# First attention in halves of the queries, first FFN begun on half the tokens, weights in thirds: one change to a fused attention and FFN kernel on one core

## The chip, the cores and the metric

The kernel runs on one core of a Trainium2 chip. The metric is the device time of one execution in microseconds (us). Every execution also has a span (first to last instruction of the core) and a mean granted clock of the matmul engine; the time was 1.9 us above the span in the profiled execution of the kernel before (472.68 against 470.8 us). "PE" is the matmul engine, "ACT" the scalar engine, "DVE" the vector engine, "POOL" the GpSimd engine and "SP" the sync engine, which here only issues DMAs.

## The reference

Eight batches of attention with 12 heads, 448 tokens and head size 64, in which the softmax has one more term in its denominator (a score of zero). Its output, as 3584 tokens of width 768, goes through an RMS normalisation and a gated FFN of inner width 1536.

```python
s = scale * q @ k.T                                   # 8 x 12 x 448 x 448
e = exp(s - m)
x = (e / (e.sum(-1) + exp(-m) + 1e-9)) @ v            # -> 3584 x 768
xn = x / sqrt(mean(x * x) + 1e-6) * rms_g
g, val = xn @ w_gate, xn @ w_val                      # 768 -> 1536
out = (g * sigmoid(g) * val) @ w_out                  # 1536 -> 768
```

## The kernel before

A batch is 448 tokens, handled as C = 4 pieces of P = 112. Heads go in pairs, six pairs a batch. For each pair q and k are transposed on PE ("turned"), four score groups are made and exponentiated on ACT, and two groups of sums (exponentials times v) follow. The first batch's attention stands alone at the start; from the second batch on, attention is woven between the FFN matmuls of earlier batches by a table of times in emission order.

```python
C = 4; P = S // C; NP = H // 2          # 4 pieces of 112 tokens, 6 pairs of heads
WB = DFF // 2                           # gate and value weights come in halves
NQPE = 7                                # groups of q, k (4 heads each) that PE turns; later ones go by DMA
stage = ctx.enter_context(tc.tile_pool(name="stage", bufs=2))     # q_f, k_f, v_f of later groups
ps_s = ctx.enter_context(tc.tile_pool(name="ps_s", bufs=2, space=bass.MemoryType.PSUM))  # scores
ps_u = ctx.enter_context(tc.tile_pool(name="ps_u", bufs=2, space=bass.MemoryType.PSUM))  # sums, turns
ps_f = ctx.enter_context(tc.tile_pool(name="ps_f", bufs=2, space=bass.MemoryType.PSUM))  # FFN
# ...
def emit_T(g):                          # turn a pair
    n, j = divmod(g, PG)
    ps = ps_u.tile([128, 2, C, P], BF16, name="qkt_ps", tag="u")
    # ... 16 transposes
    t = pair_bufs[g % 3]                # a tile for each pair
    nc.vector.tensor_copy(out=t[:, :, 0:S], in_=ps.rearrange("p i c t -> p i (c t)"))
    pair_t[g] = t
# ...
def ahead(n, jj):                       # loads of groups three ahead, on SP's queue
    n += AHEAD
    if NPE * NG + NG <= n < B * NG:     # from group 9 on
        if jj == 0:
            for i in range(3):
                load_qkv(n, i, nc.sync)
# ...
def warm(n):                            # n dummy matmuls
    ps = ps_f.tile([128, 512], FP32, name="warm_ps", tag="f")
    for _ in range(n):
        nc.tensor.matmul(ps, lhsT=blank[:, 0:128], rhs=blank, start=True, stop=True)
# ...
    warm(10)
    emit_T(0)
# ...
    between = {                         # what follows each group of scores (pair, piece)
        (0, 0): [lambda: emit_T(1)],
        (0, 1): [gains, lambda: [load_qkv(2, i, G) for i in range(2)], lambda: warm(1)],
        (0, 2): [lambda: cast_qkv(0, 2, V), lambda: load_qkv(2, 2, G), lambda: warm(1)],
        (0, 3): [lambda: warm(1)],
        (1, 0): [lambda: warm(1)],
        (1, 1): [lambda: emit_AV(0, 0)],
        # ...
    }
    for g in range(NP):
        for c in range(C):
            scores(g, c)()
            for f in between[g, c]:
                f()
    emit_AV(NP - 1, 0)
    emit_AV(NP - 1, 1)
    scale_w(1, A)
    emit_root(0)                        # 1 / rms of all 448 tokens
    # ...
    warm(14)
    for c in range(C):
        emit_scale(0, c)
    # ... turns of x, weights scaled by the gain; then the FFN
```

The softmax here doesn't subtract the row's maximum and nothing guards it: scores larger than these inputs give would overflow.

## Time and profile before

| | before |
|---|---|
| time, median of 3 | 475.81 us (473.4 to 476.49) |
| span of the profiled execution (its time: 472.68 us) | 470.8 us |
| PE busy | 456.7 us, 97% |
| the 24 exponentials of the first batch | 7.95 to 27.78 us |
| first FFN matmul | at 35.57 us |
| from there to the end of the span | 435.2 us |

The page of the kernel before: first its busy times, then busy tenths of PE in 40 slices of 11.8 us, and the granted clock in the same slices.

```profile
PE 456.7 (97%) x4048; PEld 246.7 (52%) x4048; DVE 241.1 (51%) x621; ACT 249.1 (53%) x365; POOL 95.8 (20%) x109
...
PE   7989998999999999999999989999999999999996
...
PEclk9999999999999999999999999999999999999999
```

The matmul engine is the limit nearly everywhere. The few slices below 9 are the start and the tail, and the start is what the change is about.

The timeline of ACT of the kernel before, 7 to 29 us. Columns: start, duration, engine, line, operation, out<-in, count; in brackets, idle time just before and what ended it.

```profile
7.95 3.34 ACT L210 ACTIVATE p_sb_108<-s_ps 112x896 bf16<-112x896 f32 x4 [4.30 <-PE s_ps L205]
11.17 3.35 ACT L210 ACTIVATE p_sb_111<-s_ps 112x896 bf16<-112x896 f32 x4
14.36 3.39 ACT L210 ACTIVATE p_sb_114<-s_ps 112x896 bf16<-112x896 f32 x4
...
24.44 3.34 ACT L210 ACTIVATE p_sb_114<-s_ps 112x896 bf16<-112x896 f32 x4 [0.22 <-PE s_ps L205]
```

Four exponentials take 3.22 us from one line's start to the next, with hardly any brackets: ACT is the limit of the first 28 us (busy 19.6 of the 19.8 us from 7.95 to 27.78), and PE has some slack (18.4 us busy). After the last exponential another 7.8 us pass before the FFN begins (last sums, squares, root, scalings, transposes).

### The profile page before, as it was taken

Reading aid. Unit: us, or ns where it says so; the run is one execution under the profiler, and the core shown is the slowest. Engines: PE = TensorE matmul, PEld = TensorE weight load, DVE = VectorE, ACT = ScalarE, POOL = GpSimd, SP = SyncE. Lnnn points to the kernel's source line nnn. Section 1 sums busy time; section 2 is a strip of 40 time slices with the busy share of each in tenths; the row PEclk is TensorE's granted clock in tenths of the full one; section 3 lists DMA queues with packets and bytes.
Section 4 is the critical chain, followed back from the end, with each engine's and each line's share of the span. In section 5 each row is a group of like instructions: output and inputs, shape, how many; then the busy total and the mean of one; then the engine's idle time right before and its main releaser. Section 6 shows DMA issues by size and latency. Waiting matters only on the chain.

```text
span 470.8 us, 9822 instructions
## 1 busy us (share of the span) xinstructions
PE 456.7 (97%) x4048; PEld 246.7 (52%) x4048; DVE 241.1 (51%) x621; ACT 249.1 (53%) x365; POOL 95.8 (20%) x109
## 2 busy tenths in 40 slices
PE   7989998999999999999999989999999999999996
PEld 3644544555555554544555544545455555555563
DVE  5676699455541276656532166755643247555200
ACT  4977764656555665545456555555556652222221
POOL 8424455123020222131011210313000000000000
PEclk9999999999999999999999999999999999999999
DMA  8999974998099894693069796289015221100133
GB/s 134 225 227 190 209 189 101 233 240 156 1 221 170 225 194 114 121 227 66 0 145 194 198 203 144 52 176 181 4 36 127 69 68 24 36 1 0 36 100 100
DMA packets 86776, 60.47 MB, mean 128 GB/s; under 512 B 50646, under 2 KB 81692, under 8 KB 86732
## 3 DMA queue, kind: packets, MB, share of 16 engines
q1 hardware_dynamic: 73820, 43.60, 42.5%
q0 software_dynamic: 12912, 16.26, 18.6%
q8 instruction: 31, 0.51, 0.5%
q14 instruction: 13, 0.11, 0.1%
HBM read 47.19 MB, written 11.01 MB: 124 GB/s over the span
## 4 chain that ended last, share of the span: by engine, by line
PE 85%; DVE 9%; ACT 4%; issue 1%; POOL 0%; DVEq 0%; ACTq 0%
PE o_ps L334 24%; PE v_ps L309 21%; PE g_ps L309 16%; PE u_ps L235 9%; PE s_ps L205 8%; PE s_ps L309 5%; DVE xsq L261 3%; DVE x_sb L239 1%; ACT p_sb_108 L210 1%; DVE ht_sb L320 1%; PE warm_ps L353 1%; ACT t_sb L313 1%; PE qkt_ps L178 1%; ACT p_sb_114 L210 1%; DVE x_sb L266 1%
## 5 line engine op out<-in xcount | busy, mean ns | idle before, releaser
L309 PE MATMUL v_ps<-xnt_sb,wv_bf 128*128 128x448 bf16 x576 | 125.0, 353 | 2.4 <-DVE ht_sb L320 2.4
L334 PE MATMUL o_ps<-wo_bf,ht_sb 128*128 128x384 bf16 x672 | 116.5, 326 | 0.0
L309 PE MATMUL g_ps<-xnt_sb,wg_bf 128*128 128x448 bf16 x444 | 96.4, 353 | 0.7 <-DVE silu_4291 L315 0.6
L334 PEld LDWEIGHTS <-ht_sb 128*128 128x128 bf16 x672 | 62.6, 98 | 46.2 <-issue 7.8
L309 PEld LDWEIGHTS <-wv_bf 128*128 128x128 bf16 x576 | 52.8, 97 | 54.5 <-issue 10.9
L309 PEld LDWEIGHTS <-wg_bf 128*128 128x128 bf16 x576 | 52.2, 97 | 54.2 <-issue 11.2
L313 ACT ACTIVATE t_sb<-g_ps 128x448 f32<-128x448 f32 x74 | 40.3, 544 | 68.7 <-PE g_ps L309 68.6
L210 ACT ACTIVATE p_sb_108<-s_ps 112x896 bf16<-112x896 f32 x64 | 55.5, 915 | 15.6 <-PE s_ps L205 15.5
L210 ACT ACTIVATE p_sb_114<-s_ps 112x896 bf16<-112x896 f32 x64 | 56.0, 919 | 11.8 <-PE s_ps L205 11.8
L337 ACT ACTIVATE out_sb<-o_ps 128x384 f32<-128x384 f32 x56 | 27.5, 491 | 65.6 <-PE o_ps L334 56.2
L210 ACT ACTIVATE p_sb_111<-s_ps 112x896 bf16<-112x896 f32 x64 | 55.7, 918 | 9.5 <-PE s_ps L205 9.5
L238 DVE RECIPROCAL recip<-u_ps 112x4 f32<-112x4 f32 x96 | 17.0, 177 | 82.7 <-PE u_ps L235 82.7
L239 DVE TENSOR_TENSOR x_sb<-u_ps,recip 112x256 bf16<-112x256 f32 x96 | 40.7, 424 | 3.3
L154 POOL CAST q_bf<-q_f 112x1024 bf16<-112x1024 f32 x17 | 17.7, 1040 | 102.7 <-DMA q_f<-in_q_dram 83.9
L292 POOL TENSOR_TENSOR rinv<-ms,neghalf 112x4 f32<-112x4 f32 x8 | 8.3, 1032 | 146.4 <-DVE ms L286 141.5
L205 PE MATMUL s_ps<-qk_t 64*128 64x448 bf16 x272 | 37.5, 354 | 0.0
L261 DVE CUSTOM_DVE_ANT_0 xsq<-x_sb 112x256 bf16<-112x256 bf16 (+3 forms) x62 | 35.2, 568 | 1.6
L313 ACT ACTIVATE t_sb<-s_ps 128x448 f32<-128x448 f32 x22 | 12.0, 544 | 38.5 <-PE s_ps L309 33.3
L309 PE MATMUL s_ps<-xnt_sb,wg_bf 128*128 128x448 bf16 x132 | 28.6, 352 | 0.0
L235 PEld LDWEIGHTS <-p_sb_114 112*128 112x128 bf16 (+1 forms) x512 | 19.8, 97 | 6.7 <-issue 1.4
L235 PEld LDWEIGHTS <-p_sb_111 112*128 112x128 bf16 (+1 forms) x512 | 20.0, 97 | 5.7 <-issue 1.2
L235 PEld LDWEIGHTS <-p_sb_108 112*128 112x128 bf16 (+1 forms) x512 | 19.3, 98 | 6.8 <-issue 2.8
(278 smaller groups left out, 383.0 us busy)
## 6 DMA issues: line engine op xcount, KB each, us to landing
q_f<-in_q_dram SPq DMA_DIRECT2D x15, 448.0 KB, 5.0
k_f<-in_k_dram SPq DMA_DIRECT2D x15, 448.0 KB, 6.3
v_f<-in_v_dram SPq DMA_DIRECT2D x15, 448.0 KB, 7.4
v_f<-in_v_dram POOLq DMA_DIRECT2D x9, 448.0 KB, 9.1
out_dram<-out_sb SPq DMA_DIRECT2D x8, 336.0 KB, 2.8
wg_bf<-in_moe_w_gate_dram POOLq DMA_DIRECT2D x2, 1152.0 KB, 16.5
wv_bf<-in_moe_w_val_dram POOLq DMA_DIRECT2D x2, 1152.0 KB, 14.3
wo_bf<-in_moe_w_out_dram POOLq DMA_DIRECT2D x3, 768.0 KB, 14.9
```

Source lines behind the costliest of these rows:

```text
L154: eng.tensor_copy(out=dst, in_=staged[n, i].rearrange("p h c d -> p c h d"))
L205: nc.tensor.matmul(s_ps[:, hh, 0:S], lhsT=k_t[r, k0:k0 + 128], rhs=qs[r], start=True, stop=True)
L210: nc.scalar.activation(out=p_v, in_=s_ps[0:P, :, 0:S], func=AF.Exp, scale=scale)
L235: nc.tensor.matmul(u_ps[:, qc, :], lhsT=p_sb[0:K, q0:q0 + 128], rhs=v_sb[0:K, c, h, :], start=(c == 0), stop=(c == C - 1))
L238: nc.vector.reciprocal(out=recip, in_=u_ps[0:P, :, D:E1])
L239: nc.vector.tensor_tensor(out=x_tiles[b][:, :, h * D:(h + 1) * D], in0=u_ps[0:P, :, 0:D], in1=recip.to_broadcast([P, C, D]), op=ALU.mult)
L261: nc.vector.tensor_tensor_reduce(out=xsq[:, 0:n], in0=x_c, in1=x_c, scale=1.0, scalar=0.0, op0=ALU.mult, op1=ALU.add, accum_out=acc)
L292: nc.gpsimd.tensor_tensor(out=rinv, in0=ms, in1=neghalf, op=ALU.pow)
L309: nc.tensor.matmul(ps[:, 0:S], lhsT=w[:, dk, m * 128:(m + 1) * 128], rhs=xnt_tiles[b][:, :, dk, :], start=(dk == 0), stop=(dk == KD - 1))
L313: nc.scalar.activation(out=t, in_=ps[:, 0:S], func=AF.Tanh, scale=0.5)
L334: nc.tensor.matmul(o_ps[:, 0:HN], lhsT=ht_tiles[b2][:, fk, c * 128:(c + 1) * 128], rhs=wo_bf[:, fk, n * HN:(n + 1) * HN], start=(fk == 0), ...
L337: nc.scalar.activation(out=o_sb[:, n * HN:(n + 1) * HN], in_=o_ps[:, 0:HN], func=AF.Copy, scale=0.5)
```

## The change

Intent: do the first batch's attention in two halves of the queries. Once half of the tokens have all heads, they are normalised, turned, and given to the FFN while the other half is finished, so that the FFN begins sooner. For this a unit of work is a pair of heads and half of the queries; k is needed by both halves, so q and k of a pair stay in a tile that two pairs share; the gate and value weights come in thirds, so that the first third is scaled in time; the sums get one PSUM buffer and the FFN three; and the second batch's attention is placed anew.

```diff
-    WB = DFF // 2
+    WB = DFF // 3
-    NQPE = 7
+    NQPE = 8
-    ps_u = ctx.enter_context(tc.tile_pool(name="ps_u", bufs=2, space=bass.MemoryType.PSUM))
-    ps_f = ctx.enter_context(tc.tile_pool(name="ps_f", bufs=2, space=bass.MemoryType.PSUM))
+    ps_u = ctx.enter_context(tc.tile_pool(name="ps_u", bufs=1, space=bass.MemoryType.PSUM))
+    ps_f = ctx.enter_context(tc.tile_pool(name="ps_f", bufs=3, space=bass.MemoryType.PSUM))
@@ def turned(n):
-            nc.vector.memset(qkt[n][:, :, LQ:], 0.0)
+            nc.vector.memset(qkt[n] if n < NG else qkt[n][:, :, LQ:], 0.0)
@@ def emit_T(g):
-        ps = ps_u.tile([128, 2, C, P], BF16, name="qkt_ps", tag="u")
+        ps = ps_f.tile([128, 2, C, P], BF16, name="qkt_ps", tag="f")
+        if g < NP:
+            dst = turned(n)[:, :, 0:LQ].rearrange("p i (c j t) -> p i c j t", c=C, j=PG)
+            for i in range(2):
+                nc.vector.tensor_copy(out=dst[:, i, :, j, :], in_=ps[:, i, :, :])
+            return
@@ new: scores of two key pieces for one half of the queries, sums of one half
+    def scores_half(g, h, cp, k):
+        # ... four matmuls of 224 columns, one exponential of 896 columns
+    def sums_half(g, h, k):
+        u_ps = ps_u.tile([128, 2, 2, E1], FP32, name="u_ps", tag="u")
+        # ... 16 matmuls, then reciprocal and multiply into x_sb on DVE
+    def emit_A_half(mm, part, h):
+        # ... two blocks of 128 FFN columns for 224 tokens in one PSUM buffer: 12 matmuls
@@ the x turns of the second half, and weights, now behind the FFN's start (cut)
+    ops.append((3.3, lambda: (emit_turn_x(0, 2), emit_turn_x(0, 3))))
-    for j, t0 in enumerate((0.0, 2.3, 4.9, 7.5, 11.6, 14.2, 18.4, 22.5)):
+    for j, t0 in enumerate((4.5, 7.0, 13.0, 14.5, 15.8, 17.1, 20.0, 25.5, 30.5, 36.0)):
         ops.append((t0, lambda j=j: emit_T(NP + j)))
@@ the first batch: twelve units instead of six pairs
+    units = [(0, 0), (1, 0), (0, 1), (1, 1), (2, 0), (3, 0), (2, 1), (4, 0), (5, 0), (3, 1), (4, 1),
+             (5, 1)]
     between = {
+        (2, 1): [lambda: sums(0)],
+        (3, 0): [lambda: sums(1)],
+        (3, 1): [lambda: emit_T(2), lambda: load_w(2), lambda: cast_qkv(1, 2, G)],
+        (4, 0): [lambda: emit_T(3)],
+        # ...
+        (10, 1): [lambda: emit_turn_x(0, 0), lambda: emit_stats(0, 0, (3,))],
+        (11, 0): [lambda: sums(10), lambda: emit_turn_x(0, 1)],
+        (11, 1): [lambda: scale_w(2, V)],
     }
+    # ... after the last unit: sums, squares and root of the second half
+    warm(6)
```

## The prediction

> **What bounds it now.** The matmul engine: 456.7 of 470.8 us busy, the chain of waits 85% on it. From 85 us to the tail it idles 2.5 us (busy time by stretch: 368.5 of 371), so three places can give: the first 35.6 us, 35.6 to 85, and the tail.
>
> - 7.9 to 27.8 (timeline): the first batch's 24 exponentials run back to back on the scalar engine, 0.81 us apart. It is busy 19.6 of 19.9 us.
> - 27.8 to 35.6 (timeline, chain of waits): last sums, squares, root (1.15 us on GpSimd), scalings, transposes, 14 dummy matmuls. The first FFN matmul is at 35.57.
> - 35.6 to 85: FFN and second batch's attention. Its pieces (24 groups of six at 1.14, 14 score groups at 0.48, 12 sums at 0.50, 13 turns) sum to 46 of 49.5 us.
> - Tail: last eviction ends at 466.7, span at 470.8: one output DMA.
>
> **What changes.** The first half of the queries is normalised, scaled and turned while the last exponentials run. FFN work on it follows after some weight scaling and six dummies: about 2.2 us after the last exponential instead of 7.8. Gross gain about 5.5 us. [...]
>
> **What it costs.**
> 1. Each turned pair is now copied into a shared tile whose two pairs interleave; the built program makes the next scores wait for that copy, even for the other pair. Turn 0.51 + copy about 0.7 + scores 0.3 + latencies = 1.7 us (from the trace) against 0.8 per exponential: five such places, 0.5 to 0.9 us each. The last exponential moves from 27.8 to about 30 to 31.5. This eats 2 to 4 us of the gain.
> 2. Work moved behind the FFN's start: two transposes of the second half (0.8 us) and one turn (0.5).
> 3. Two more turns on the matmul engine: 1.0 us.
> 4. Second batch's attention is squeezed: about 26 us of matmul work against about 25 us scalar and 26 us vector. Loss 0 to 2 us over before.
>
> **Gains beside.** Three instead of two FFN PSUM buffers: most of the 2.4 us that matmuls waited for ht/silu. Output tail by halves: about 0.7 us. One buffer for the sums should be harmless later (1.6 us of other matmul work lies between sums). Weights in thirds should arrive in time (210 GB/s now).
>
> Sum: -5.5 +3 +1.3 +1.0 +0.5 (squeeze) -2 -0.7, so about -2.5 to -3. All of it is on the critical path.
>
> **Predicted: 473.0 us, 468.5 to 477.0 (80%). Faster by over 2%: 0.04; within 2%: 0.93; slower: 0.03.**
>
> **What would show it.** First FFN matmul at 32 to 34 us (35.6 before), about 2 us after the last exponential. Scalar idle of 2 to 4 us between the first 24 exponentials, released by scores that waited for the qk_t copies. Waits for ht_sb on matmuls near zero. Tail after last eviction near 3.4 us.
>
> **What would make it wrong.** If copies hide under the scores' two buffers, the first FFN matmul comes at 30 and the time is about 470. If the squeezed stretch stalls (vector engine's queue, single sums buffer), or third weights or keys land late, 476 to 478.

The terms as they stand come to -2.4 us, recorded as about -2.5 to -3.

## More of the kernel before

The timeline of PE of the kernel before, from the start.

```profile
1.20 4.45 PE L353 MATMUL warm_ps<-blank 128*128 128x512 bf16 x10 [1.20 <-DVE blank L65]
5.58 0.58 PE L178 MATMUL qkt_ps<-identity,q_bf 112*64 112x112 bf16 x8
...
7.54 0.36 PE L205 MATMUL s_ps<-pair_t_102 64*128 64x448 bf16 x2 [1.01 <-DVE pair_t_102 L181]
```

Ten dummy matmuls, a first turn, 1.01 us idle, then scores. The same turn of eight takes 0.58 us here and 0.36 to 0.39 from 7.84 us on: the array is at half rate at first. The durations show it (so do the ten dummies here, 0.445 us each, where the 14 at 28.76 us took 0.228); the granted clock row does not (it gives 1.00 from time zero).

Waits of PE in the kernel before, 36 to 125 us (us in total, times, longest).

```profile
PE v_ps L309 <- DVE ht_sb L320: 0.9, 3, 0.4
PE u_ps L235 <- DVE pair_t_102 L181: 0.6, 1, 0.6
PE xnt_ps L275 <- DVE x_sb L266: 0.4, 1, 0.4
PE s_ps L205 <- DVE pair_t_106 L181: 0.2, 1, 0.2
```

Once the FFN runs, PE waits about 2 us in 89.

## The result, and the profile after

| | before | after |
|---|---|---|
| time, median | 475.84 us (4 runs) | 496.0 us (4 runs, 495.17 to 497.31) |
| span | 470.8 us | 494.0 us |
| last of the first 24 exponentials ends | 27.78 us | 47.12 us |
| first FFN matmul | 35.57 us | 50.47 us |
| first FFN matmul to end of span | 435.2 us | 443.5 us |

The ratio is 1.0435 (95% interval 1.0399 to 1.0472): slower. Ratios are the mean time of one kernel's fast runs over that of the other's of the same rounds, so not quite the ratio of the medians quoted. The prediction of 473.0 us, and its range up to 477.0, are missed by far.

In the two traces the loss has two parts: 14.9 us before the first FFN matmul, where a gain of about 2.5 was expected, and 8.3 us after it, where nothing or a small gain was expected. Together 23.2 us of span.

The page of the kernel after, the same lines.

```profile
PE 466.8 (94%) x4169; PEld 255.6 (52%) x4169; DVE 248.8 (50%) x644; ACT 250.8 (51%) x362; POOL 96.1 (19%) x110
...
PE   6777988779999999999999999999999999999996
...
PEclk9975999999999999999999999999999999999999
```

The hole is in the first eight slices (12.35 us each). The granted clock falls in the third and fourth. No slice of the profile before had that.

ACT's timeline of the kernel after, 10 to 47 us.

```profile
10.80 0.92 ACT L251 ACTIVATE p_sb_108<-s_ps 112x896 bf16<-112x896 f32 x1 [6.20 <-PE s_ps L247]
13.04 0.92 ACT L251 ACTIVATE p_sb_108<-s_ps 112x896 bf16<-112x896 f32 x1 [1.32 <-PE s_ps L247]
...
30.95 0.92 ACT L251 ACTIVATE p_sb_108<-s_ps 112x896 bf16<-112x896 f32 x1 [1.77 <-PE s_ps L247]
...
46.20 0.92 ACT L251 ACTIVATE p_sb_110<-s_ps 112x896 bf16<-112x896 f32 x1 [1.12 <-PE s_ps L247]
```

One exponential costs what it did (0.92 us; 915 to 919 ns on the page before). Nearly each now has a bracket: ACT waits for scores. The first starts 2.85 us late. From the first exponential to the last ACT is busy 21.9 of 36.3 us (19.6 of 19.8 before): it idles 14.4 us, where the prediction had 2 to 4. PE is busy 26.4 of them, so the limit has gone from ACT to PE and the waits in front of PE.

The first DMAs of SP's queue, after (before, the first line was the only one in the first 20 us):

```profile
0.75 0.38 SPq L570 DMA_DIRECT2D rms_rows<-in_moe_rms_g_dram  x1
1.20 0.35 SPq L151 DMA_DIRECT2D q_f<-in_q_dram  x1
1.58 0.48 SPq L151 DMA_DIRECT2D k_f<-in_k_dram  x1
```

These are q and k of group 9, 448 KB each, needed much later. In the old program they were third in line for a pool of two buffers and waited for the pool. With NQPE at 8 one group fewer passes through that pool, group 9 finds a free buffer, and its DMAs start at 1.20 us (80.20 us before), ahead of q and k of the very first pair, of which q is issued at 1.30 us. PE's timeline from the start shows the result:

```profile
7.66 0.58 PE L186 MATMUL qkt_ps<-identity,q_bf 112*64 112x112 bf16 x8 [2.02 <-DMA q_bf<-in_q_dram]
...
8.81 1.46 PE L432 MATMUL warm_ps<-blank 128*128 128x512 bf16 x3
10.21 0.56 PE L247 MATMUL s_ps<-qk_t 64*128 64x224 bf16 x4
```

The first turn is 2.08 us late, and the scores at 10.21 take 0.56 us for what takes 0.36 at full rate.

Later in the same timeline:

```profile
28.31 0.36 PE L186 MATMUL qkt_ps<-identity,k_bf 112*64 112x112 bf16 x8
30.48 0.36 PE L247 MATMUL s_ps<-qk_t 64*128 64x224 bf16 x4 [1.81 <-DVE qk_t L191]
...
31.02 0.59 PE L186 MATMUL qkt_ps<-identity,k_bf 112*64 112x112 bf16 x8
32.39 0.55 PE L247 MATMUL s_ps<-qk_t 64*128 64x224 bf16 x4 [0.79 <-DVE qk_t L191]
```

The scores at 30.48 waited 1.81 us for a copy into the shared tile; DVE was filling (memset) other tiles meanwhile, the last of them the shared tile of the next two pairs:

```profile
28.51 0.82 DVE L169 MEMSET qk_t<- 128x912 uint32 x1
...
29.74 0.68 DVE L191 COPY qk_t<-qkt_ps 128x448 bf16<-128x448 bf16 x2
```

The turn behind it is already slow (0.59 us at 31.02 for the 0.36 of 28.31), and the array runs at half rate from there, until about 50 us.

PE's waits, after, 7 to 51 us, then 51 to 125 us:

```profile
PE s_ps L247 <- DVE qk_t L191: 5.0, 5, 1.8
PE u_ps L264 <- DVE x_sb L269: 2.1, 5, 0.5
PE qkt_ps L186 <- DMA q_bf<-in_q_dram: 2.0, 1, 2.0
PE xnt_ps L328 <- DVE x_sb L319: 1.6, 1, 1.6
...
```

```profile
PE xnt_ps L328 <- DVE x_sb L319: 2.1, 1, 2.1
PE u_ps L288 <- DVE x_sb L292: 1.6, 3, 0.9
PE s_ps L218 <- ACT p_sb_110 L223: 1.4, 4, 0.4
PE v_ps L361 <- DVE wv_bf L129: 1.3, 2, 1.0
PE v_ps L361 <- ACT wv_bf L127: 0.9, 1, 0.9
PE g_ps L361 <- DVE xnt_sb L333: 0.8, 1, 0.8
...
```

In the second stretch the waits listed for the kernel after sum to 9.9 us (with the four lines cut, of 0.6, 0.5, 0.5 and 0.2), against 2.1 before. The waits for ht_sb are gone, as predicted; others have come. The 12 matmuls of 224 columns are innocent: a group starts at 52.09 and the next at 53.24, so one takes 96 ns, about half of the 190 ns of one of 448 columns before (six from 35.57 to 36.71 us). Only the very first group was still at half rate (50.47 to 52.09, 1.62 us).

### The profile page after: what moved, and what is told of

Its sections match the earlier page's. It is cut to its first block, busy times and chain, and to the rows that moved or that the text cites. A ratio compares the mean times of both kernels' runs of the same rounds, so it can differ in the third digit from the quotient of the medians.

```text
span 494.0 us, 10113 instructions
## 1 busy us (share of the span) xinstructions
PE 466.8 (94%) x4169; PEld 255.6 (52%) x4169; DVE 248.8 (50%) x644; ACT 250.8 (51%) x362; POOL 96.1 (19%) x110
## 4 chain that ended last, share of the span: by engine, by line
PE 88%; DVE 5%; ACT 3%; DMA 1%; issue 1%; POOL 0%; ACTq 0%; POOLq 0%
PE o_ps L411 23%; PE v_ps L361 21%; PE g_ps L361 16%; PE u_ps L288 8%; PE s_ps L218 7%; PE s_ps L361 5%; PE u_ps L264 2%; PE s_ps L247 2%; PE warm_ps L432 1%; PE qkt_ps L186 1%; DMA k_bf<-in_k_dram 1%; PE g_ps L384 1%; DVE qk_t L191 1%; DVE xsq L314 1%; DVE x_sb L269 1%
## 5 line engine op out<-in xcount | busy, mean ns | idle before, releaser
L361 PE MATMUL v_ps<-xnt_sb,wv_bf 128*128 128x448 bf16 x552 | 120.3, 353 | 2.7 <-DVE wv_bf L129 1.3
L361 PE MATMUL g_ps<-xnt_sb,wg_bf 128*128 128x448 bf16 x420 | 91.2, 353 | 0.8 <-DVE xnt_sb L333 0.8
L361 PEld LDWEIGHTS <-wv_bf 128*128 128x128 bf16 x552 | 50.2, 98 | 52.9 <-issue 7.9
L223 ACT ACTIVATE p_sb_110<-s_ps 112x896 bf16<-112x896 f32 x56 | 49.4, 916 | 10.8 <-PE s_ps L218 10.8
L223 ACT ACTIVATE p_sb_109<-s_ps 112x896 bf16<-112x896 f32 x56 | 48.9, 915 | 10.2 <-PE s_ps L218 10.2
L291 DVE RECIPROCAL recip<-u_ps 112x4 f32<-112x4 f32 x84 | 14.8, 177 | 75.2 <-PE u_ps L288 75.2
L223 ACT ACTIVATE p_sb_108<-s_ps 112x896 bf16<-112x896 f32 x56 | 48.8, 915 | 7.6 <-PE s_ps L218 7.3
L345 POOL TENSOR_TENSOR rinv<-ms,neghalf 112x4 f32<-112x4 f32 (+1 forms) x9 | 8.6, 959 | 159.9 <-DVE ms L343 133.6
L162 POOL CAST q_bf<-q_f 112x1024 bf16<-112x1024 f32 x16 | 16.7, 1042 | 106.6 <-DMA q_f<-in_q_dram 90.9
L292 DVE TENSOR_TENSOR x_sb<-u_ps,recip 112x256 bf16<-112x256 f32 x84 | 35.7, 424 | 3.2 <-DMA q_f<-in_q_dram 0.4
L314 DVE CUSTOM_DVE_ANT_0 xsq<-x_sb 112x512 bf16<-112x512 bf16 (+1 forms) x61 | 35.0, 574 | 1.6
L218 PE MATMUL s_ps<-qk_t 64*128 64x448 bf16 x256 | 35.3, 354 | 0.0
L288 PEld LDWEIGHTS <-p_sb_110 113*128 113x128 bf16 x448 | 17.5, 97 | 6.1 <-DVE x_sb L292 1.9
L288 PEld LDWEIGHTS <-p_sb_108 113*128 113x128 bf16 x448 | 17.0, 97 | 6.8 <-issue 1.9
L288 PEld LDWEIGHTS <-p_sb_109 113*128 113x128 bf16 x448 | 17.5, 97 | 5.5 <-issue 1.1
```

The costliest lines, as they stand in the source:

```text
L162: eng.tensor_copy(out=dst, in_=staged[n, i].rearrange("p h c d -> p c h d"))
L218: nc.tensor.matmul(s_ps[:, hh, 0:S], lhsT=k_t[r, k0:k0 + 128], rhs=qs[r], start=True, stop=True)
L223: nc.scalar.activation(out=p_v, in_=s_ps[0:P, :, 0:S], func=AF.Exp, scale=scale)
L288: nc.tensor.matmul(u_ps[:, qc, :], lhsT=p_sb[0:K, q0:q0 + 128], rhs=v_sb[0:K, c, h, :], start=(c == 0), stop=(c == C - 1))
L291: nc.vector.reciprocal(out=recip, in_=u_ps[0:P, :, D:E1])
L292: nc.vector.tensor_tensor(out=x_tiles[b][:, :, h * D:(h + 1) * D], in0=u_ps[0:P, :, 0:D], in1=recip.to_broadcast([P, C, D]), op=ALU.mult)
```

## The experiments

The theory after reading: three independent holdups of PE (the early loads; the tile shared by two pairs; one buffer for the sums) each leave PE idle for 0.4 to 2 us, the array's rate halves on such idleness, and at half rate PE's work for one exponential exceeds ACT's 0.81 us, so PE becomes the limit. The trace of before shows two rates: its first ten dummies took 0.445 us each, the 14 at 28.76 us 0.228. That idleness brings the lower one was the theory at this point, and the runs below test it. Rivals: one of the holdups alone does it; the rate is a bystander; and for the loss behind the FFN's start, that the second batch's attention is packed too densely.

Eighteen kernels were run. The summary, with the ratio to before in its own rounds; "rest" is the span from the first FFN matmul to the end.

| run | based on | median us | ratio (95%) | first FFN matmul | rest |
|---|---|---|---|---|---|
| before | | 475.8 | | 35.57 | 435.2 |
| after | | 496.0 | 1.044 (1.040, 1.047) | 50.47 | 443.5 |
| hold | after | 494.0 | 1.042 (1.039, 1.045) | 48.33 | 443.6 |
| early_before | before | 477.2 | 1.007 (1.004, 1.010) | 39.07 | 436.0 |
| dummies | after | 491.1 | 1.036 (1.033, 1.040) | 44.54 | 444.3 |
| hold_pairs | after | 490.1 | 1.034 (1.029, 1.038) | 45.24 | 443.4 |
| u2 | after | 499.6 | 1.052 (1.048, 1.057) | 44.09 | 453.1 |
| hold_pairs_u2 | after | 492.1 | 1.036 (1.032, 1.040) | 37.14 | 453.4 |
| spread | after | 497.6 | 1.048 (1.044, 1.051) | 50.24 | 443.8 |
| fix | hold_pairs_u2 | 488.3 | 1.029 (1.025, 1.034) | 35.79 | 450.5 |
| fix_u | fix | 483.8 | 1.020 (1.016, 1.023) | 35.42 | 445.2 |
| fix_u_w | fix_u | 481.2 | 1.016 (1.012, 1.021) | 36.65 | 443.0 |
| best | fix_u_w | 477.8 | 1.007 (1.004, 1.010) | 34.57 | 441.4 |
| best_w | best | 478.3 | 1.008 (1.005, 1.011) | 34.10 | 442.0 |
| tail_before | before | 475.0 | 1.001 (0.998, 1.003) | 37.90 | 435.0 |
| before_cold | before | 474.9 | 1.001 (0.998, 1.004) | 38.17 | 435.5 |
| before_warm | before | 472.9 | 0.996 (0.994, 0.999) | 35.55 | 435.7 |
| hold_dummies | after | 491.5 | 1.036 (1.033, 1.038) | 46.12 | 443.8 |
| hold_u2 | after | 495.5 | 1.044 (1.040, 1.048) | 42.30 | 451.5 |
| before_u1 | before | 477.4 | 1.007 (1.004, 1.011) | 39.27 | 435.7 |

The first FFN matmul and the rest come from one trace of each, so small steps in these two columns are not clear of scatter. Kernels that are the same up to the first FFN matmul show how much: after and spread differ by 0.2 us, best and best_w by 0.5, fix_u and fix_u_w by 1.2, before and tail_before by 2.3.

### The early loads: hold and early_before

hold puts the q and k of group 9 on GpSimd's queue, where they come late (after 100 us):

```diff
                 for i in range(3):
-                    load_qkv(n, i, nc.sync)
+                    load_qkv(n, i, G if n == NPE * NG + NG and i < 2 else nc.sync)
```

> The changed kernel, with the first two loads of the hardware DMA queue (queries and keys of the tenth group, 448 KB each) issued from GpSimd's queue in their turn instead of at 1.2 us. Theory EARLY LOADS (they compete with the first queries and keys and so start the clock's fall): the first turn begins near 5.6 us instead of 7.66, the first exponential near 8 instead of 10.8, the granted clock is 1.00 up to 20 us; at the least 3 to 5 us come back (491 to 493 us). If the second clock drop (29 to 52 us) hangs on that first one too, the first FFN matmul is at 37 to 39 instead of 50.5 and the time 481 to 484. Theory SHARED TILE alone (idle behind the copies of turned pairs is the cause): the second drop stays, 491 to 493. If neither, 496.

early_before gives the old kernel the early loads: q and k of group 7 are asked for on SP's queue, where nothing holds them.

```diff
-                 (14.3, lambda: (cast_qkv(NG + 2, 2, G), loads(2 * NG + 1))),
+                 (14.3, lambda: (cast_qkv(NG + 2, 2, G), load_qkv(2 * NG + 1, 0, nc.sync),
+                         load_qkv(2 * NG + 1, 1, nc.sync), load_qkv(2 * NG + 1, 2, G))),
```

> The kernel before, with the queries and keys of the eighth group issued from the hardware DMA queue, where nothing holds them back, instead of from GpSimd's queue: it puts the same two early loads into the old kernel. Theory EARLY LOADS: first turn at about 7.6 instead of 5.6 us, half clock from about 9 to 17 us, time 3 to 5 us longer (479 to 481). If only the landing is late and the clock holds, plus 2 us. If the early loads do not matter, the time stays within 0.5 us of before.

In hold the first turn came at 5.25 us, as early as before, yet the first FFN matmul came only 2.1 us sooner. PE's timeline of hold says why:

```profile
12.18 0.37 PE L247 MATMUL s_ps<-qk_t 64*128 64x224 bf16 x4
14.03 0.68 PE L264 MATMUL u_ps<-v_sb,p_sb 113*128 113x65 bf16 x16 [1.48 <-DVE x_sb L269]
...
14.93 0.47 PE L186 MATMUL qkt_ps<-identity,q_bf 112*64 112x112 bf16 x8
15.18 0.59 PE L186 MATMUL qkt_ps<-identity,k_bf 112*64 112x112 bf16 x8
16.56 0.55 PE L247 MATMUL s_ps<-qk_t 64*128 64x224 bf16 x4 [0.79 <-DVE qk_t L191]
```

With the first cause gone, the next took its place: sums waited 1.48 us for the single buffer to be emptied (DVE was filling tiles), and the rate halved within 1 us. In the changed kernel the array was at full rate from 17 us until 30.8. In the old kernel the early loads left PE idle for 1.6 us before the first turn, the clock fell, and the FFN started at 39.07; the time rose by 0.7%. The expectation held there (rate at half from 9.3 to 16 us, 3.3 us more than the median of its rounds), though not the 479 to 481 us. Of hold's, only the early turn did: 494.0 us is above its 491 to 493, and the clock fell at 15 us. In the timed runs hold (1.042) cannot be told from after (1.044). So the early loads are shown to cost by early_before; that they take about 2 us in the changed kernel is the reading of one trace of each. The rest of the span of early_before stayed at 436.0.

### Is it the rate? dummies, hold_dummies, before_cold, before_warm

dummies keeps the array busy with matmuls of nothing, 19 instead of 10 at the start and 3 or 7 behind each turn:

```diff
-    warm(10)
+    warm(19)
     emit_T(0)
-        (3, 1): [lambda: emit_T(2), lambda: load_w(2), lambda: cast_qkv(1, 2, G)],
+        (3, 1): [lambda: emit_T(2), lambda: warm(3), lambda: load_w(2), lambda: cast_qkv(1, 2, G)],
         # the same behind emit_T(1), emit_T(3) and emit_T(5); warm(7) behind emit_T(4)
```

> The changed kernel with more dummy matmuls and nothing else: 19 instead of 10 at the start, three more behind each turned pair of the first batch (seven behind the fifth). Theory CLOCK (the idle itself is short; the halved clock that follows it is what costs): granted clock 1.00 or close to it up to 50 us, the first FFN matmul at 38 to 42 instead of 50.5 us, time 484 to 488. If the idle waits themselves are the cost, more work on the matmul engine cannot help: 495 to 500.

The granted clock stayed at 1.00 until 40 us, and the FFN started 5.9 us earlier although PE had more to do. So the rate is not a bystander here. But 44.5 and 491.1 us lie between the ranges of both theories, and 44.5 is far from 33: the waits for tiles hold the exponentials at full rate too, and the dummies cost time themselves.

hold_dummies is both edits together.

> The changed kernel with the ninth group's q and k put back on GpSimd's queue (as in hold) and the extra dummies (as in dummies). If early loads and lost matmul rate are two separate causes and together most of the late FFN start, the first FFN matmul comes at 38 to 42 (50.5 changed, 48.3 hold, 44.5 dummies), the rest of the span stays at 443 to 445, time 484 to 488. If the shared tile's waits and the single sums buffer are what holds the exponentials whatever the rate, it stays at 43 to 45 and the time at 489 to 491.

It started the FFN at 46.12, later than dummies, and missed both ranges for that point. Nineteen dummies were sized for late loads; with loads in time they stand in front of the first turn (first exponential at 9.76 us instead of 7.03 in hold), and the clock fell anyway, at 16.7 us, behind a wait of 1.27 us for the sums buffer. (In dummies the same wait of 1.27 us, at nearly the same place, lost nothing.) The time of 491.5 is just above where the second theory had put it. Dummies treat a symptom, and blindly added ones are work.

before_cold takes the single dummies out of the old kernel's first scores, and nothing else:

```diff
-        (0, 2): [lambda: cast_qkv(0, 2, V), lambda: load_qkv(2, 2, G), lambda: warm(1)],
-        (0, 3): [lambda: warm(1)],
-        (1, 0): [lambda: warm(1)],
+        (0, 2): [lambda: cast_qkv(0, 2, V), lambda: load_qkv(2, 2, G)],
+        (0, 3): [],
+        (1, 0): [],
         # likewise behind (0, 1), (2, 0), (3, 0) and (5, 0)
```

> The kernel before without the six single dummy matmuls among its first scores, nothing else changed. Theory (a short stretch with an idle matmul engine at the start keeps or drops its rate, and a slow matmul engine then holds up the exponentials): matmuls in 8 to 20 us run slower, the last exponential ends 0.5 to 4 us later than 27.8, first FFN matmul at 36 to 39, rest of the span as before (435 to 436); time 1 to 3 us above before. Rival (the rate of the matmuls does not matter in this kernel, the scalar engine has slack to hide it): last exponential at 27.8, time within 0.5 us. A fall that feeds itself, as in the changed kernel, would show as an FFN start past 42.

(The expectation says six; the edit takes out seven.) Busy times by stretch, PE first and the granted clock before the last two columns:

```profile
5.00:10.00 5.00, 3.02 (x39) 1.58 (x36) 3.11 (x8) 1.41 (x2) 3.79 (x8) 0.75 1.11 184
10.00:15.00 5.00, 4.18 (x44) 2.12 (x41) 1.43 (x3) 4.48 (x6) 3.06 (x5) 0.50 1.29 226
15.00:20.00 5.00, 5.00 (x78) 3.16 (x77) 2.58 (x7) 3.97 (x6) 1.64 (x3) 0.73 1.15 231
```

In this trace about 10 us run at half rate; the last exponential ends at 30.39 instead of 27.78, the first FFN matmul comes at 38.17, 2.6 us late, and the span is 2.9 us longer. Then it recovers: the old order has no other holdup that would feed the loss. So lost rate alone costs 2 to 3 us, not 15.

But it was not the missing dummies that lost it. PE's timeline of before_cold:

```profile
1.19 3.73 PE L353 MATMUL warm_ps<-blank 128*128 128x512 bf16 x10 [1.19 <-DVE blank L65]
4.85 0.39 PE L178 MATMUL qkt_ps<-identity,q_bf 112*64 112x112 bf16 x8
...
7.53 0.55 PE L205 MATMUL s_ps<-pair_t 64*128 64x448 bf16 x2 [1.98 <-DVE pair_t L181]
```

The first scores are at half rate already, ahead of the first dummy taken out. The same ten dummies took 3.73 us here and 4.45 in the profile of before: the array got to full rate sooner, was done sooner, and then idled 1.98 us instead of 1.01 for the copy that comes at 7.5 in either case. So the point at which full rate comes differs between executions of the same start. In a third trace of this start (tail_before, below) the dummies took 4.32 us, the gap was 1.51 us, and the array was at half rate from 8.8 us.

The timed runs gave a ratio of 1.0006, and that too is about the kernel before. Its executions come with their granted clock, and the twelve of these rounds sort themselves: the four with a mean clock of 0.999 took 472.68 to 473.54 us, the three with 0.996 to 0.998 took 474.08 to 474.26, and the five with 0.990 to 0.992 took 474.93 to 476.22. The old kernel seems to lose rate in most executions, and in the traces of the variants that start as it does (before_cold, tail_before) it is at this gap. Its profiled execution, 470.8 us with a clock of 1.000, was one of the lucky ones, so the prediction started from a first stretch some 2 us better than usual. (This also is why the medians differ by 20.2 us and the spans by 23.2.)

before_warm adds three dummies to the old kernel, in this gap:

```diff
     warm(10)
     emit_T(0)
+    warm(3)
```

> The kernel before with three more dummy matmuls after the first turn of q and k. Theory (the old kernel stands near the edge of losing its matmul rate at the start, and loses it in some executions): time 0 to 1.5 us below before, with less spread. Rival (the dummies only stand in the way of the first scores): 0 to 1.5 us above before.

Six executions of 472.1 to 473.34 us, all with a clock of 0.998 to 1.000, idle time before the first scores 0.78 us: ratio 0.9964 (0.9942 to 0.9987). That is 0.36% and well under a per cent, but the interval excludes 1. It is the only version here that beat the kernel before, and the test of the reading above.

How long an idle time loses the rate is not fixed in these runs. fix_u and fix_u_w (below) are the same program up to the first FFN matmul, and in both a turn of x waits 1.73 us. PE's timeline of fix_u, then of fix_u_w:

```profile
29.41 0.47 PE L323 MATMUL xnt_ps<-identity,x_sb 112*128 112x112 bf16 x6 [1.73 <-DVE x_sb L314]
...
29.00 0.74 PE L323 MATMUL xnt_ps<-identity,x_sb 112*128 112x112 bf16 x6 [1.73 <-DVE x_sb L314]
```

In fix_u the turn ran at full rate, and the granted clock fell 2.3 us after the wait, at 31.7 us; in fix_u_w it fell within the wait, at 28.2. The FFN started at 35.42 and 36.65. Which of the two an execution gets is luck as far as these runs tell.

### The shared tile and the sums buffer: hold_pairs, u2, hold_u2, hold_pairs_u2

hold_pairs gives each pair its own tile again, as before, on top of hold. DVE's fills of the whole shared tiles (0.82 us each) go with them, so the step below is that of the tiles and their fills together:

```diff
-        if g < NP:
-            dst = turned(n)[:, :, 0:LQ].rearrange("p i (c j t) -> p i c j t", c=C, j=PG)
-            for i in range(2):
-                nc.vector.tensor_copy(out=dst[:, i, :, j, :], in_=ps[:, i, :, :])
-            return
         t = pair_bufs[g % 3]
@@ scores_half
-        qs = qkt[n][:, 0, 0:LQ].rearrange("p (c j t) -> p c j t", c=C, j=PG)[:, 2 * h:2 * h + 2, j, :]
+        qs = pair_t[g][:, 0, 2 * h * P:(2 * h + 2) * P]
-            k0 = ((2 * cp + cc) * PG + j) * P
+            k0 = (2 * cp + cc) * P
-                                 lhsT=qkt[n][r, 1, k0:k0 + 128], rhs=qs[r], start=True, stop=True)
+                                 lhsT=pair_t[g][r, 1, k0:k0 + 128], rhs=qs[r], start=True, stop=True)
```

> As hold, and each turned pair of the first batch is copied into a tile of its own, as the kernel before does (three tiles in turn are enough); the whole-tile memsets go with it. Theory SHARED TILE on top of EARLY LOADS: three of the five waits of scores for copies go, the last exponential ends at 29 to 31 us instead of 47.1, no half clock, first FFN matmul at 32 to 34, time 478 to 482. If the single sums buffer is what starves the scalar engine in the first attention, the last exponential stays beyond 33 and the time above 486.

u2 gives the changed kernel two sums buffers and two for the FFN and the turns, nothing else:

```diff
-    ps_u = ctx.enter_context(tc.tile_pool(name="ps_u", bufs=1, space=bass.MemoryType.PSUM))
-    ps_f = ctx.enter_context(tc.tile_pool(name="ps_f", bufs=3, space=bass.MemoryType.PSUM))
+    ps_u = ctx.enter_context(tc.tile_pool(name="ps_u", bufs=2, space=bass.MemoryType.PSUM))
+    ps_f = ctx.enter_context(tc.tile_pool(name="ps_f", bufs=2, space=bass.MemoryType.PSUM))
```

> The changed kernel with two PSUM buffers for the attention sums and two for the FFN, as before the change. Theory SINGLE SUMS BUFFER (with one buffer each second sum waits for the vector engine, 0.44 us or more each time; this keeps the matmul engine under-used and the clock at half): the waits of sums for x_sb vanish, first FFN matmul at 46 or earlier instead of 50.5, time at most 492. If the clock falls all the same by the early loads and the copies: gain under 2.5 us (494 to 496).

hold_pairs_u2 joins the three edits (hold, own tiles, two sums buffers).

> hold_pairs with two sums buffers as well: all three suspects of the first attention undone. In hold_pairs the clock fell at about 14 us, right after 1.15 us of waiting for the one sums buffer. If those three together are the cause, the granted clock stays 1.00 to 40 us, the last exponential ends at 29 to 31, the first FFN matmul is at 32 to 34 (45.2 in hold_pairs), time 476 to 479. If the clock still falls, the first FFN matmul is beyond 40.

hold_u2 is hold with two sums buffers, and so differs from hold_pairs_u2 in the shared tiles and their fills alone.

> The changed kernel with the early q and k loads held back and two buffers for the sums (two for the FFN and the turns), its first batch still turned into the shared tiles. It differs from hold_pairs_u2 (first FFN matmul at 37.1) in the shared tiles alone. If these cost what the prediction said (2 to 4 us on the last exponential) and no more, the FFN starts at 39 to 41. If they cost more, because the waits of up to 2 us at the matmul engine halve its rate as well, 42 to 44. If nothing, 37 to 38, and the early loads and the single sums buffer explain all. Rest of the span 453, time 493 to 498.

Own tiles on top of hold (hold to hold_pairs) bring the FFN's start from 48.33 to 45.24, not to the expected 32 to 34; the rate still fell at about 14 us, behind a wait of 1.15 us for the sums buffer, and the branch that named this buffer came true (time above 486). Two sums buffers alone (after to u2) bring it from 50.47 to 44.09, as expected; the time of 499.6 was not. Put one upon the other they form a ladder, in which the steps depend on the order taken:

| undone, one upon the other | first FFN matmul | step |
|---|---|---|
| nothing (after) | 50.47 | |
| early loads (hold) | 48.33 | -2.1 |
| single sums buffer (hold_u2) | 42.30 | -6.0 |
| shared tiles (hold_pairs_u2) | 37.14 | -5.2 |

Three edits take back 13.3 of the 14.9 us. The last of them, hold_pairs_u2, still missed its expectation (32 to 34 us, clock 1.00 to 40 us): the clock fell at about 29 us, while a turn of x waited 1.73 us. The waits for shared tiles in hold_u2 (PE, 5 to 40 us) were these, the longest (2.17 us, before the scores at 23.76 us) at the place where in after DVE was filling a whole tile:

```profile
PE s_ps L247 <- DVE qk_t L191: 5.9, 5, 2.2
```

The granted clock in 20 to 30 us was 0.76 in hold_u2 and 0.96 in hold_pairs_u2. PE waited 1.9 us for copies of turned pairs in hold_pairs_u2, against these 5.9. So the waits seem to be most of the step, and the rate part of it. The start of the FFN at 42.30 was in the range of the theory that both act.

But the time hardly moved (492.1 us in hold_pairs_u2, 490.1 in hold_pairs): with two FFN buffers the rest of the span grew from 443.5 to 453. Turns of pairs and of x had been moved by the change into the FFN's pool, and two buffers are too few for both.

### The rest of the span: spread, before_u1, fix, fix_u, fix_u_w

spread places the second batch's pairs evenly, in case the dense placing was what cost:

```diff
-    for j, t0 in enumerate((4.5, 7.0, 13.0, 14.5, 15.8, 17.1, 20.0, 25.5, 30.5, 36.0)):
+    for j, t0 in enumerate((4.5, 7.0, 10.2, 12.8, 15.2, 17.4, 20.0, 25.5, 30.5, 36.0)):
-    for j, t0 in enumerate((5.6, 8.6, 14.1, 15.5, 16.9, 18.3)):
-        ops += [(t0 + 0.34 * i, op) for i, op in enumerate(micro_ops(NP + j))]
+    for j, t0 in enumerate((5.6, 8.2, 10.8, 13.4, 16.0, 18.3)):
+        ops += [(t0 + (0.34 if j == 5 else 0.6) * i, op) for i, op in enumerate(micro_ops(NP + j))]
```

> The changed kernel, only the second batch's attention is spread evenly over the first FFN (a pair each 2.6 us of the plan instead of two pairs, a pause and four pairs each 1.4). Theory SQUEEZE (scalar and vector engine are overloaded in the dense part): the 443.5 us from the first FFN matmul to the end fall to 439 to 441, time 492 to 494. If the loss lies in the halves themselves and the moved turns, it stays at 443 to 444 and the time at 496.

The rest was 443.8 against 443.5. Placing them evenly gained nothing; the theory that the density is the cause, which the prediction had named as a risk, falls.

before_u1 gives the old kernel the change's PSUM buffers, and nothing else:

```diff
-    ps_u = ... bufs=2 ...
-    ps_f = ... bufs=2 ...
+    ps_u = ... bufs=1 ...
+    ps_f = ... bufs=3 ...
     # the turns of pairs, x and gain take their buffers from ps_f
```

> The kernel before with only the PSUM buffers of the change: one for the sums, three for the FFN and all turns. The prediction called one sums buffer harmless later and the third FFN buffer a gain of about 2 us. If both hold, the rest of the span falls from 435.2 to about 433 and the FFN starts 0.5 to 4 us late (waits of 0.44 us for the sums at each pair); time within 2 us of before. If the single sums buffer is what slows the second batch's attention in the changed kernel, the rest of the span is 437 to 441 and the time 477 to 482.

The rest was 435.7: neither gain nor loss. PE's waits of before_u1, 36 to 120 us:

```profile
PE u_ps L235 <- DVE x_sb L239: 2.3, 3, 1.1
PE g_ps L309 <- DVE ht_sb L320: 1.8, 1, 1.8
...
```

This is neither of the two ranges expected. So "one buffer for the sums is harmless later" holds within a microsecond in the old order, and the third FFN buffer is worth nothing measurable: the waits for ht_sb went from 2.4 to 1.8 us over the whole span, and those for the sums buffer came. The FFN started 3.7 us late; the clock fell at the start in this trace too (0.75 in 5 to 10 us).

fix takes hold_pairs_u2 and moves fills and turns ahead:

```diff
     set_v(0)
+    set_p(1)
     warm(10)
-        (0, 0): [lambda: emit_T(1), lambda: set_p(1)],
+        (0, 0): [lambda: emit_T(1), lambda: set_p(2)],
-        (1, 1): [lambda: warm(1), lambda: set_p(2)],
+        (1, 1): [lambda: warm(1)],
-        (3, 0): [lambda: sums(1)],
-        (3, 1): [lambda: emit_T(2), lambda: load_w(2), lambda: cast_qkv(1, 2, G)],
+        (3, 0): [lambda: emit_T(2)],
+        (3, 1): [lambda: sums(1), lambda: load_w(2), lambda: cast_qkv(1, 2, G)],
         # and emit_T(4) before sums(5) instead of behind it
```

> hold_pairs_u2, with the memsets of the weights' tiles moved ahead of the first scores and two turns one exponential earlier. If vector-engine work in front of the sums' evictions and late turns are what remains: 1 to 2 us better than hold_pairs_u2, first FFN matmul at 30.5 to 32.5, time 474 to 477; the 443.5 us from the first FFN matmul to the end, equal in all variants of the changed kernel so far (435.2 before), should stay within 1 us, so no gain over before.

(The text calls them the weights' tiles; what is filled earlier are the exponentials' tiles.) The exponentials ran from 7.5 to 32.4 us, the granted clock was 1.00 until 30 us, and the FFN started at 35.79: 1.35 us sooner than hold_pairs_u2, and still not sooner than before. All three expectations were missed: the start, the time (488.3) and the rest (450.5). One stall stood out: the last scores sit behind a turn of x that waited 1.7 us for its scaling. In the trace the turn starts at 28.88 us, behind 1.73 us of idle time, and the scores emitted behind it at 29.28 us, with no wait of their own.

fix_u takes the turns' buffers back to the sums' pool, as before the change:

```diff
-        ps = ps_f.tile([128, 2, C, P], BF16, name="qkt_ps", tag="f")
+        ps = ps_u.tile([128, 2, C, P], BF16, name="qkt_ps", tag="u")
         # the same for xnt_ps and r_ps
```

> fix, with the turned pairs and the turned x back in the sums' two PSUM buffers, as before the change, so that only the FFN uses its two. In fix the first FFN matmul came at 35.8 us (35.6 before) and yet the time was 488, because the stretch from there to the end took 450.5 us, against 443.5 in the changed kernel and 435.2 before. Theory FFN BUFFERS (two buffers shared with turns hold the FFN up): that stretch falls to 442 to 445, time 480 to 482. If two FFN buffers alone are too few for halves: it stays near 450, time 487 to 489.

The rest fell from 450.5 to 445.2, and the time by 4.5 us to 483.8, both just above the range. So 5.3 us of a loss like u2's (about 10 us) come from turns and FFN sharing two buffers; the other half is not traced to one cause.

fix_u_w scales the second and third thirds of the weights earlier:

```diff
-        ops.append((6.0 + 0.4 * i, lambda: scale_w(1, V)))
-        ops.append((9.0 + 0.2 * i, lambda i=i: scale_w(1, (V, A)[i % 3 == 2])))
+        ops.append((5.0 + 0.3 * i, lambda: scale_w(1, V)))
+        ops.append((7.0 + 0.3 * i, lambda i=i: scale_w(1, (V, A)[i % 3 == 2])))
         # likewise 16.0 and 18.2 to 14.2 and 16.5
```

> fix_u, with the scaling of the second and third thirds of the weights begun 1 to 2 us of the plan earlier. Theory LATE SCALING (with thirds, scaling falls due sooner, and the matmuls wait 2.2 us for it): those waits (v_ps for wv_bf) fall below 0.5 us and the stretch from the first FFN matmul to the end by 1.5 to 2.5 us. If the vector and scalar engine are full there anyway, other waits grow and the time stays within 0.5 us of fix_u.

The waits for wv_bf (1.5 and 0.9 us in fix_u) were gone, and the rest fell by 2.2 us, as expected. The timed runs do not yet separate the two kernels (1.016 to 1.023 and 1.012 to 1.021).

### Versions meant to win: best, best_w, tail_before

best moves the first half's turns of x behind the last scores, with three dummies fewer, and the second batch's x turns 0.7 us later:

```diff
-        (10, 1): [lambda: emit_turn_x(0, 0), lambda: emit_stats(0, 0, (3,))],
-        (11, 0): [lambda: sums(10), lambda: emit_turn_x(0, 1)],
+        (10, 1): [lambda: emit_stats(0, 0, (3,))],
+        (11, 0): [lambda: sums(10)],
@@ after the last unit
+    emit_turn_x(0, 0)
+    emit_turn_x(0, 1)
     sums(11)
@@
-    warm(6)
+    warm(3)
-        ops.append((23.2 + 1.0 * c, lambda c=c: emit_turn_x(1, c)))
+        ops.append((23.9 + 0.8 * c, lambda c=c: emit_turn_x(1, c)))
```

> fix_u_w, with the first half's x turned after the last scores instead of ahead of them in the matmul engine's order (three dummies fewer), and the second batch's turns of x 0.7 us later in the plan. Theory IN-ORDER TURN (scores queue behind a turn that waits 1.7 us for the normalised half): the last exponential ends 2 to 3 us earlier (32.4 in fix), first FFN matmul at 33 to 34, time 2 to 3 us below fix_u_w, about 475 to 477. If the chain of sums, root and scaling decides the start anyway, no change.

The last exponential ended at 31.53 (32.4 in fix) and the FFN started at 34.57, both short of what was expected; the time of 477.8 just missed its range. It is 18 us faster than the changed kernel and still 0.7% slower than before. Its idea works as drawn, and the head start is 1.0 us; the rest is 6.2 us longer than before.

best_w asks for the last third of the weights earlier, because DVE was seen waiting 2.0 us for it:

```diff
+                 (4.6, lambda: load_w(2)),
-                 (7.1, lambda: (loads(NG + 2), load_w(2), cast_qkv(NG + 1, 2, G))),
+                 (7.1, lambda: (loads(NG + 2), cast_qkv(NG + 1, 2, G))),
```

> The repaired kernel (best) with the third third of the gate and value weights asked for 2.5 us of FFN work earlier, ahead of a group of q, k and v. The vector engine waited 2.0 us for them at 58 to 60 us. If that wait held matmuls, the rest of the span falls from 441.4 by 0.5 to 2 us, time 475.8 to 477.3, within 0.5 per cent of before. If the loads of q, k, v that now come later hold the turns of the second batch, no gain or 1 us worse.

No gain: rest 442.0 against 441.4, ratio 1.008 against 1.007. DVE's wait was off PE's path.

tail_before is the old kernel with the change's last edit alone, the last output written in two halves:

```diff
-        if n == 1:
+        last = b2 == B // 2 - 1 and c == 6
+        if n == 1 or last:
+            cols = slice(n * HN, (n + 1) * HN) if last else slice(0, DM)
```

> The kernel before, with the last output written in two halves of the columns as the changed kernel does, and nothing else. All theories: 0.4 to 1.0 us faster (the last DMA is half as large), the distance from the last eviction to the end 3.2 to 3.7 us instead of 4.1.

From the last eviction's end to the end of the span: 4.1 us before, 3.9 here, 3.5 in the changed kernel. The distance is above the 3.2 to 3.7 expected, and in the time nothing can be measured (1.0007, 0.9984 to 1.0029).

## Why the prediction was wrong

**The start of the FFN** was predicted at 32 to 34 us and came at 50.47.

- The prediction took for granted that the first exponential starts when it did before. It started 2.85 us late. Two loads for later use had lost the buffer wait that had held them back, and went ahead of the first q and k. Undone, the FFN starts 2.1 us sooner in the trace (hold); given to the old kernel, they cost 0.7% (early_before). The step was missing altogether, and it lay in plain sight: one number for a pool's users had changed, and the first loads on an idle queue are the ones to look at. With these two loads ahead the first turn came at 7.66 us, without them at 5.58 (before) and 5.25 (hold).
- "Each turned pair is now copied into a shared tile": the mechanism was right. There were five waits, four of them of 0.79 us and so within the predicted 0.5 to 0.9; the fifth was 1.81 us, because DVE was filling tiles at that moment, and they sum to 5.0 us. With the other two holdups undone, the shared tiles and their fills are worth 5.2 us of the FFN's start (hold_u2 to hold_pairs_u2), where 2 to 4 had been put down; with one sums buffer left, 3.1 (hold to hold_pairs).
- "One buffer for the sums should be harmless later": it was judged for the later stage only, and there it holds (before_u1). In the first attention only one group of scores (0.30 us) stands between two sums, where the prediction had 1.6 us of other work, and the second buffer was worth 6.0 us (hold to hold_u2).
- Matmul durations were taken from a trace at full rate; that they could change was no term of the sum. In stretches with idle times of 1.2 to 2.0 us the array went to half rate in most of these traces. Then PE's work for an exponential takes longer than the exponential. In the old kernel about 10 us of this cost 2.6 us (before_cold) and end by themselves; in the changed kernel each fall is followed by another wait, and the last 20 us before the FFN all ran at half rate (granted clock 0.50 from 31 to 50.47 us). An estimate from the traces of after and before_cold: per exponential, one group of scores (0.30 us to the next start at full rate, 0.49 at half), half a group of sums (0.60 and 0.99) and a quarter of a turn (0.52 and 0.89) make 0.73 us at full rate and 1.21 at half, against ACT's 0.81. With the rate kept up, its FFN starts 5.9 us sooner (dummies).
- A turn of x was put in front of the last scores. It waits for a root and a scaling, and the scores behind it came only after it (in after the turn at 42.83 us, behind 1.58 us of idle time, the scores at 43.50): 1.6 us more.

These sizes overlap and are not to be added: a wait that also loses the rate is counted in both. What is shown is that the three holdups, undone together, take back 13.3 of 14.9 us in the traces, and that repaired further (best) the FFN starts at 34.57, half a microsecond outside the predicted range. "About 2 us after the last exponential" measured 3.35 us after the change and 3.04 in best.

**The rest of the span** was predicted to lose 1.3 + 1.0 + 0 to 2 and to gain 2 + 0.7, so to stay even. It lost 8.3 us.

- The work moved behind the FFN's start and the two more turns measured about 2.4 us (0.8 for two turns of x, 0.6 for a pair, 1.0 for two more pairs). That term was right.
- The squeeze as such is not the loss (spread: no difference). What the traces show in its place: weights scaled too late (2.2 us of the rest regained in fix_u_w), a turn of the second batch's x that waits 2.1 us, sums and exponentials that wait for each other. Only the first of these was tested by itself.
- The gain from three FFN buffers did not come: the waits for ht_sb did vanish, and others took their place. In the old order the buffers alone changed nothing (435.7 against 435.2).
- The output by halves is 0.6 us in one trace, and not measurable in the time.

What stays open: about 3 of the 6.2 us by which the rest of best exceeds that of before. Moved work explains 2.4. The FFN of best also starts at half rate: its first group takes 1.90 us until the next starts, where one at full rate takes 1.15, so 0.75 us more. PE's waits in 36 to 120 us sum to 5.1 us in best against 1.8 before, which would fill the remainder, but no run took these waits away one by one.

**The base.** The profile before was of an execution without loss of rate. By their clocks and times, most executions of that kernel do lose some, about 2 us; that the profiled one did not was luck.

## What to carry to other kernels

A change that frees a buffer or shortens a queue's list also changes when loads start: list the first DMAs of every queue, before and after, and ask what they now precede. Where an engine other than PE is the limit, PE has idle times, and here these lost the rate of its array: they then cost twice, once as waits and once as slower matmuls (0.49 instead of 0.30 us for a group of scores). So cost such a stage at both rates, and do not rely on one trace of it: the same wait of 1.73 us kept the rate in one execution and lost it in another. And judge "one buffer fewer is harmless" for every stage that uses the pool, above all for the one in which little else runs between two uses.

## What these runs show of the array's rate

- The array was at half rate within about 2.5 us of single idle times of 2.0 us (before_cold), 1.8 (after), 1.6 (early_before), 1.5 (hold, tail_before), 1.3 (hold_dummies) and 1.15 us (hold_pairs), each in a stretch that was less than fully busy, and in best within 1 us of an idle time of 0.65 us (before 29.14 us; PE was busy 7.4 us of 20 to 30 us). It held its rate after 1.01 us (the profiled run of before) and 0.78 us (before_warm), but also after 1.27 us (dummies) and 1.37 us (hold_u2). So no single length decides; how much is the gap, how much the busy share around it and how much the moment at which it falls, these runs don't tell.
- The profile's granted clock can miss the low rate at the start: in before the dummies at 1.20 us took 0.445 us each, and turns at 5.58 us 0.58 us for eight, with the row at 1.00; at full rate eight take 0.36 to 0.39.
